# Delta-rule attention, two expert stages and a dense stage on one core: the first two chunks inverted one at a time, x reordered by on-chip transfers, four raw weight buffers at the start

## The chip, the core and the metric

The kernel runs on one core of one Trainium2 chip. The metric is the device time of one execution in microseconds (us). The core has five engines that run their own instruction lists and wait for each other by semaphores: PE (matrix products, its weight loads shown apart as PEld), DVE, ACT and POOL (elementwise work) and SP, which here only issues transfers. 16 DMA engines carry the transfers.

## The reference

Three stages follow one another. The first is a recurrence over 768 time steps for 4 x 8 heads of width 48; the second is a mixture of eight experts whose weights per token come from eight rounds of row and column scaling; the third is a dense product.

```python
for t in range(S):                     # S = 768, state is D x D per head, D = 48
    y[:, :, t] = einsum(q[:, :, t], state)
    v_old = einsum(state, kt)          # kt is k[t] over its norm plus 1e-6
    state = state + bt * outer(kt, vt - v_old)
x = y as (3072 tokens, 384)
P = exp(x @ w_gate - max); 8 rounds of row and column scaling
out = sum over 8 experts e of P[:, e] * (relu(x @ w1[e]) @ w2[e])     # 384 -> 1024 -> 384
result = ((out @ a1) * (out @ a2)) @ w3 @ w_out                      # 384 -> 1024 -> 1024 -> 384
```

## The kernel before

**Phases.** The time axis is cut into 12 chunks of 64 steps, c = 0 to 11. In phase A (about the first 405 us) the chunks are solved one after the other and expert 0 is computed for each chunk's 256 tokens as soon as its x is there. Phase B does experts 1 to 7 in three passes over the tokens, phase C the dense stage; both need nothing of a chunk's order beyond x itself.

**One chunk of phase A.** `prep_k` (L508) forms the Gram products of k on PE, squares k on ACT, and on DVE sums the squares and turns beta into beta over the squared norm (L521 to L538, tiles `nrm`, `bm`, `nv`). The recurrence inside a chunk is a unit triangular 64 x 64 system per head. `invert` (L588) inverts two chunks (a pair j) at once: DVE transposes `a` so that each partition holds one 32 x 32 block (L599), multiplies by beta, does forward substitution for the 8 x 8 blocks by 14 short instructions (L609 to L614), joins them by the pairs of a product and a sum in `prod` (L616 to L626, a 512-element product and a 512-element sum at a time, later 1024), and transposes back. For the pairs j = 1 to 5 it goes on up to 32 x 32 (L670, L672) and `tt_make` joins the halves to 64 x 64 on PE. For j = 0 it stops at 16 x 16 blocks, and `substitute` (L729) forms on PE the matrix R that is left over; in `seq` three products with R (written `rv`, PE reading `xst`) and a sum on DVE after each (`u<-b,vs`) finish the solution. Before the change, chunks 0 and 1 come out of one inversion.

**From the chunk to expert 0.** `seq` (L787) multiplies the solution into y (`pt,u` on PE), and ACT copies y to the tile `xst` in on-chip memory. Its rows are per head. Two transfers then write it to the DRAM tensor `xs_d`, which is in the order of the model's features, and `xload` (L779) reads it back as three blocks of 128 features:

```python
self.dma(lambda b=b: T["xs_d"][c].rearrange("h (j q e) t -> q e (h j) t", q=2, e=D)[b], ...)   # two of them
self.dma(raw, lambda: self.T["xs_d"][c].rearrange("h (k p) t -> p (h k) t", p=128), ...)       # and back
```

ACT copies that to `xr` as a high part, and POOL or DVE subtracts to get the low part. `e0` (L916) does expert 0 with it: 72 products of `xr` by `wA` and 72 of `hA` by `wA` for a chunk. `xr` has two buffers, so chunk c + 2 can be loaded only once the 72 `xr` products of chunk c are done.

**Expert 0's weights.** `load_w` (L984) loads eight blocks into two raw buffers in turn (`yr` and `wraw`), ACT copies each to the high part in `wA`, and POOL subtracts the low part in one instruction of 768 elements.

**The order of the work.** It is not written out by hand. `Plan.order` places every operation by its priority, a cost and latencies, and each engine then runs its list strictly in that order. While PE has nothing to do before the first chunk's expert work, the planner puts in products of a zero tile `wz` (up to 400, `setup`), which compute nothing. The fillers stop once an expert 0 product with a priority from 200 on is placed. A transfer is issued by SP in SP's order, so one that waits holds up the next.

Of the kernel before, what the change touches and what calls it, by code (L numbers as in the profile page):

```python
# [20 lines left out]
D = 48  # L21
# [27 lines left out]
SUB = 2  # L49
FLAT = "p a b c d -> p (a b c d)"  # L50
# [28 lines left out]
class Plan:  # L79
# [58 lines left out]
    WARM = 20.0  # L138
    SEED = 32
    PASS_BY = .05  # L140
# [238 lines left out]
class Kernel:  # L379
# [56 lines left out]
    def setup(self):  # L436
        nc, T, g = self.nc, self.T, self.g
        n = NCH * NG
        self.open("const", "left", ones=((128, 128), F32), masks=((128, 78), F32),
# [16 lines left out]
                  asys=((128, 1056), F32), t=((128, 1056), F32), prod=((128, NP, 1024), F32), xs=((128, 256), F32), bm2=((128, 2, 32), F32), wz=((128, 384), F16),  # L456
# [14 lines left out]
        g.op({"POOL": .2}, lambda e: nc.gpsimd.memset(T["t"].rearrange("p (i x) -> p i x", x=33)[:, :, 0:1], 1.0), w=["t"], prio=-5)  # L471
        self.dma(lambda: T["wgr"], lambda: a["moe_w_gate"].rearrange("(k p) e -> p k e", p=128), 12288, [], ["wgr"], -5)
        g.op({"POOL": .2}, lambda e: nc.gpsimd.memset(T["ones"], 1.0), w=["ones"], prio=-31)
        g.op({"ACT": 1.5}, lambda e: nc.scalar.activation(out=T["nrm"][:, 1, 0:1], in_=T["ones"][:, 0:1], func=AF.Sqrt), r=["ones"], w=["n1"], prio=-30)
# [34 lines left out]
    def prep_k(self, c):  # L509
# [13 lines left out]
        if st:  # L523
            n0 = [("n0", 0), ("n0", 1)]
            bm = lambda: T["bm"][:, 32 * j:32 * j + 32]
            nv = lambda: T["nv"][:, 32 * j:32 * j + 32]
            g.op({"DVE": .1}, lambda e: nc.vector.tensor_scalar(out=nr(0), in0=nr(0), scalar1=1e-30, scalar2=None, op0=ALU.max), w=n0, prio=pr)
            g.op({"ACT": .25}, lambda e: nc.scalar.activation(out=nr(1), in_=nr(0), func=AF.Sqrt), r=n0, w=["n1"], prio=pr)
# [15 lines left out]
        if c < SUB:  # L544
            g.op({"POOL": .4}, lambda e: nc.gpsimd.memset(self.rb(c)[:, :, :, 48:64], 0.0), w=[("gm", c)], prio=-6)
# [7 lines left out]
        for hf in range(2):  # L553
# [5 lines left out]
            if c >= SUB:  # L559
                g.op({"ACT": act(256, True)}, lambda e, s=s, gs=gs, st=st: self.copy(  # L560
                    "ACT", T["g12"][:, gi, st, gs], self.ps(s, 8, 64)[:, :, 32:64], -1.0),
                    r=[s], w=[(n, gi, st, hf) for n in ("g12", "xsb0", "xsb1")], prio=pg)
            g.op({"ACT": act(256, True)}, lambda e, s=s, ss=ss, a0=a0: self.copy(
                "ACT", T["a0"][:, a0.at, ss], self.ps(s, 8, 64)[:, :, 0:32], -1.0), r=[s], w=[ak], prio=pg)
            for r in (slice(32, 64), slice(96, 128)):
                g.op({"ACT": act(256, True)}, lambda e, s=s, ss=ss, a0=a0, r=r: self.copy(
                    "ACT", T["a0"][r, a0.at, ss], self.ps(s, 8, 64)[r, :, 32:64], -1.0), r=[s], w=[ak], prio=pg)
            for i in range(3) if c < SUB else ():
                g.op({"ACT": act(128, True)}, lambda e, s=s, hf=hf, i=i: self.copy(
# [18 lines left out]
    def invert(self, j):  # L588
# [55 lines left out]
        if j == 0:  # L644
# [6 lines left out]
            for c in range(SUB):  # L651
                self.substitute(c)
# [963 lines left out]
```

## Time and profile before

| what | us |
|---|---|
| median of 3 runs (lowest, highest) | 2077.08 (2074.74, 2077.18) |
| the profiled execution, device time | 2078.16 |
| its span in the trace | 2076.4 |
| PE busy in the span | 2044.1 |
| DVE busy in the span | 1208.9 |

The span is what the profiler saw from the first to the last instruction, 1.8 us less than the device time of the same execution. Busy time of PE counts the fillers like any other product. DVE's share of the span (58%) is a mean over phases: the page's 40 slices show it at 7 to 9 tenths in the first six, which are phase A up to 311 us, and lower after them.

### The profile page before, as it was taken

Reading aid. Unit: us, or ns where it says so; the run is one execution under the profiler, and the core shown is the slowest. Engines: PE = TensorE matmul, PEld = TensorE weight load, DVE = VectorE, ACT = ScalarE, POOL = GpSimd, SP = SyncE. Lnnn points to the kernel's source line nnn. Section 1 sums busy time; section 2 is a strip of 40 time slices with the busy share of each in tenths; the row PEclk is TensorE's granted clock in tenths of the full one; section 3 lists DMA queues with packets and bytes.
Section 4 is the critical chain, followed back from the end, with each engine's and each line's share of the span. In section 5 each row is a group of like instructions: output and inputs, shape, how many; then the busy total and the mean of one; then the engine's idle time right before and its main releaser. Section 6 shows DMA issues by size and latency. Waiting matters only on the chain.

```text
span 2076.4 us, 39969 instructions
## 1 busy us (share of the span) xinstructions
PE 2044.1 (98%) x16463; PEld 1749.8 (84%) x16463; DVE 1208.9 (58%) x1947; ACT 733.1 (35%) x1438; POOL 792.4 (38%) x849
## 2 busy tenths in 40 slices
PE   7999999999999999999999999999999999999999
PEld 6898999978888888788888888788888888988888
DVE  7898882665444445756666667766666643222222
ACT  6545433343443443323333323323323322222222
POOL 1300011067666667355454454443554534200000
PEclk9999999999999999999999999999999999999999
DMA  5444323276645546755655545656546537400000
GB/s 215 133 141 130 110 73 109 72 259 234 227 173 188 212 178 223 269 174 204 220 189 175 204 152 191 239 189 208 202 164 216 188 106 208 102 31 16 16 23 24
DMA packets 166615, 331.64 MB, mean 160 GB/s; under 512 B 13409, under 2 KB 117793, under 8 KB 154913
## 3 DMA queue, kind: packets, MB, share of 16 engines
q1 hardware_dynamic: 132544, 193.82, 27.6%
q0 software_dynamic: 33888, 135.28, 19.2%
q8 instruction: 129, 2.11, 0.4%
q14 instruction: 54, 0.43, 0.1%
HBM read 235.10 MB, written 93.95 MB: 158 GB/s over the span
## 4 chain that ended last, share of the span: by engine, by line
PE 87%; DVE 5%; DMA 5%; issue 1%; POOL 1%; ACT 1%; SPq 0%; POOLq 0%; DVEq 0%; ACTq 0%
PE b L401 87%; DMA acc<-y_d 1%; DMA wo_d<-cv 1%; DVE prod L412 1%; DMA xs_d<-xst 1%; DMA xst<-xs_d 0%; DMA rawB<-in_moe_w 0%; SPq L432 0%; DMA xT<-xs_d 0%; DVE cv L415 0%; POOL acc L412 0%; DVE xs L625 0%; POOL wA L412 0%; DVE hA L415 0%; DMA xf_d<-acc 0%
## 5 line engine op out<-in xcount | busy, mean ns | idle before, releaser
L401 PE MATMUL b<-hA,wA 128*128 128x512 f32 (+1 forms) x2367 | 508.3, 353 | 5.0 <-DVE hA L415 5.0
L401 PEld LDWEIGHTS b<-hA,wA 128*128 128x128 f32 x2367 | 392.4, 189 | 67.5 <-DVE hA L415 6.2
L412 POOL TENSOR_TENSOR acc<-acc,tmp 128x512 f32<-128x512 f32 x252 | 335.8, 1334 | 195.3 <-DVE tmp L412 190.8
L401 PE MATMUL b<-hB,wA 128*128 128x512 f32 x1521 | 388.4, 391 | 0.2 <-DVE hB L415 0.2
L401 PEld LDWEIGHTS b<-hB,wA 128*128 128x128 f32 x1521 | 287.1, 189 | 60.5 <-DVE hB L415 0.6
L401 PE MATMUL b<-xr,wA 128*128 128x256 f32 (+1 forms) x1620 | 326.4, 335 | 1.5 <-POOL xr L412 1.5
L401 PEld LDWEIGHTS b<-xr,wA 128*128 128x128 f32 x1620 | 250.1, 189 | 33.9 <-POOL xr L412 1.7
L405 ACT ACTIVATE rt<-b 128x512 f32<-128x512 f32 x300 | 178.4, 598 | 257.5 <-PE b L401 252.2
L401 PE MATMUL b<-xT,wA 128*128 128x512 f32 x1008 | 249.9, 389 | 1.8 <-POOL wA L412 1.8
L412 DVE TENSOR_TENSOR b<-b,rt 128x512 f32<-128x512 f32 x252 | 173.4, 695 | 103.2 <-ACT rt L405 73.8
L401 PEld LDWEIGHTS b<-xT,wA 128*128 128x128 f32 x1008 | 189.0, 188 | 41.8 <-POOL wA L412 2.7
L412 POOL TENSOR_TENSOR cv<-cv 128x256 f32<-128x256 f32 (+3 forms) x179 | 131.9, 737 | 209.5 <-DVE cv L1376 115.8
L401 PE MATMUL b<-xT,wS 128*128 128x512 f32 x756 | 199.3, 390 | 1.4 <-ACT rt L405 1.4
L412 DVE TENSOR_TENSOR tmp<-b,pb 128x512 f32<-128x512 f32 x150 | 103.2, 689 | 137.9 <-PE b L401 133.6
L415 DVE SCALAR_TENSOR_TENSOR hA<-b,hA 128x512 fp32r<-128x512 f32 x215 | 144.2, 688 | 62.0 <-ACT hA L941 30.3
L401 PEld LDWEIGHTS b<-xT,wS 128*128 128x128 f32 x756 | 141.7, 188 | 31.8 <-ACT rt L405 2.2
L412 DVE TENSOR_TENSOR rt<-b,rt 128x512 f32<-128x512 f32 x48 | 33.2, 692 | 186.0 <-PE b L401 186.0
L415 DVE SCALAR_TENSOR_TENSOR hB<-b,hB 128x512 fp32r<-128x512 f32 x169 | 114.8, 686 | 32.8 <-ACT hB L1181 32.4
L412 DVE TENSOR_TENSOR tmp<-b,yr 128x512 f32<-128x512 f32 x102 | 70.2, 689 | 98.0 <-PE b L401 85.3
L412 POOL TENSOR_TENSOR wA<-rawB,wA 128x768 fp32r<-128x768 f32 (+1 forms) x49 | 88.6, 1818 | 100.1 <-DMA pb<-p_d 72.4
L405 ACT ACTIVATE cv<-cv 128x256 fp32r<-128x256 f32 x72 | 29.1, 404 | 272.1 <-DVE cv L415 272.1
L1181 ACT ACTIVATE hB<-b 128x512 fp32r<-128x512 f32 x169 | 100.1, 596 | 69.6 <-DVE b L412 67.5
(189 smaller groups left out, 2421.4 us busy)
## 6 DMA issues: line engine op xcount, KB each, us to landing
wA<-wq_d POOLq DMA_DIRECT2D x56, 1536.0 KB, 8.9
wq_d<-wA SPq DMA_DIRECT2D x28, 1536.0 KB, 7.1
wS<-ws_d POOLq DMA_DIRECT2D x56, 512.0 KB, 4.8
rawB<-in_moe_w SPq DMA_DIRECT2D x108, 192.0 KB, 3.4
ws_d<-wS SPq DMA_DIRECT2D x28, 512.0 KB, 6.6
w_d<-cv SPq DMA_DIRECT2D x112, 128.0 KB, 1.7
cvr<-in_w3T SPq DMA_DIRECT2D x32, 256.0 KB, 2.9
wS<-w_d POOLq DMA_DIRECT2D x32, 256.0 KB, 3.6
```

What stands on the lines that cost most here:

```text
L401: self.nc.tensor.matmul(*args, skip_group_check=True, **kw)
L405: self.nc.scalar.activation(out=out, in_=in_, func=AF.Copy, **({} if scale is None else {"scale": scale}))
L412: self.E[eng].tensor_tensor(out=out, in0=in0, in1=in1, op=op)
L415: self.nc.vector.scalar_tensor_tensor(out=out, in0=in0, scalar=scalar, in1=in1, op0=op0, op1=op1)
L1181: g.op({"ACT": actb(512)}, lambda e: nc.scalar.activation(out=hv(0), in_=self.ps(s, 512), func=AF.Relu), r=[s], w=[(out, 0, 0)], prio=pe)
```

## The change

- **Chunks 0 and 1.** `invert(0)` now calls a new function `blocks16` once for each of the two chunks, followed by `substitute`. For one chunk it transposes 512 elements, so that all partitions work on its 16 x 16 diagonal blocks, two 8 x 8 blocks each, and joins these by two pairs of product and sum in place of four. The norms and beta of chunks 0 and 1 are computed apart, 16 columns each, and a new small product `bq` puts masks on beta. R is now masked on DVE (`xst<-b,masks`) while it is copied out; before, ACT copied it and the masks were on the twelve small copies of the Gram products, of which four whole copies are left.
- **x.** y's 48 rows per head half are put into three blocks of 128 rows within `xst`: the heads' rows stay, and six small transfers move the fourth part (16 rows each, 16 KB) into the free rows. x is thus in another order of features; the rows of the gate's and of w1's matrices are permuted to match when the inputs are laid out. Expert 0 no longer waits for DRAM; `xs_d` is still written, for phase B.
- **Weights.** Four raw buffers at first (a third slot of `kraw` and of `vs` beside `yr` and `wraw`), issued earlier (priorities `WP`), and POOL's subtraction is cut in three pieces of 256 elements, which wait for the end of chunk 0's inversion.
- **The planner's constants** WARM, SEED, PASS_BY are others (20.0, 32, .05 before), so that the whole order is drawn anew.

```diff
-    WARM = 20.0
-    SEED = 32
-    PASS_BY = .05
+    WARM = 13.0
+    SEED = 26
+    PASS_BY = 0.02
...
+    def blocks16(self, c):
...
+        pr = -131.0 if c == 0 else 1.0
...
+        raw = lambda: T["asys"][:, 0:512].rearrange("p (i r) -> p i r", i=16)
...
+        g.op({"DVE": dve(512)}, port=True, fn=lambda e: self.tt(
+            e, v4(), v4(), T["bq"][:, 4:6, 16 * c:16 * c + 16].rearrange("p a (s o) -> p s a o", o=1).to_broadcast([128, 16, 2, 16]), ALU.mult),
+            r=[("bq", c)], w=ka, prio=pr)
+        g.op({"DVE": 1.0}, lambda e: nc.vector.transpose(
+            out=raw().rearrange("p i (a s) -> p i a s", a=2), in_=v4().rearrange("p s a i -> p i a s")), r=ka, w=["asys"], prio=pr)
+        g.op({"DVE": dve(256)}, port=True, fn=lambda e: self.tt(
+            e, am().rearrange("p i q -> p q i"), raw()[:, :, 0:16], raw()[:, :, 16:32], ALU.add), r=["asys"], w=[("F", c)], prio=pr)
+        for i in range(1, 8):
...
+                "DVE", pv(), blk(t16)[:, :, 0:i, 0:i],
...
     def invert(self, j):
+        if j == 0:
+            for c in range(2):
+                self.blocks16(c)
+                self.substitute(c)
+            return
...
         for hf in range(2):
-            g.op({"ACT": act(512, True)}, lambda e, hf=hf: self.copy(e, self.rb(c)[:, hf], self.ps(sr[hf], 8, 64)),
-                 r=[sr[hf], ("gmr", c)], w=[("R", c, hf)], prio=pr)
+            g.op({"DVE": dve(512)}, lambda e, hf=hf: self.tt(
+                e, self.rb(c)[:, hf], self.ps(sr[hf], 8, 64), T["masks"][:, 84:148].rearrange("p (o t) -> p o t", o=1).to_broadcast([128, 8, 64]),
+                ALU.mult), r=[sr[hf], ("gmr", c), "masks"], w=[("R", c, hf)], prio=pr)
...
-        for b in range(2):
-            self.dma(lambda b=b: T["xs_d"][c].rearrange("h (j q e) t -> q e (h j) t", q=2, e=D)[b],
...
+        for k_ in range(3):
+            for b in range(2):
+                r0, r1 = 64 * b + 16 * k_, 64 * b + 48
+                self.dma(lambda r1=r1, k_=k_: xv()[r1:r1 + 16, :, k_], lambda r0=r0: xv()[r0:r0 + 16, :, 3], 16384,
+                         [(xb, 0), (xb, 1)], [(xb, "m", k_, b)], pr + .5, lat=.9, cost=.4)
...
+        self.xload(lambda i: T["xr"][:, i, x.at], lambda: xv()[:, :, 0:3], xk, x, pr + .5)
+        for hh in range(2):
+            self.dma(lambda hh=hh: T["xs_d"][c, hh].rearrange("(k p) t -> p k t", p=128), lambda hh=hh: xv()[:, hh, 0:3], 196608,
+                     xk, [("xs", c, hh)], pr + .5)
...
+        for i in range(3):
+            g.op({"POOL": pool2(256)}, port=True, fn=lambda e, i=i: self.tt(
...
+                r=[(raw, 0), (raw, 1), ("w", sl, 0), ("t16e", 0)], w=[("w", sl, 1)], prio=prio)
...
+                    ring, nm = {2: (self.kraw, "kraw"), 3: (self.vring, "vs")}.get(n, (self.wraw, None))
```

Three places of the changed order follow, as the two lists have them; the numbers after the names are the tiles' numbers.

**DVE, chunk 0 from the scaled beta to the end of the inversion.** Before, for both chunks at once (the 14 short instructions and four of the pairs stand between):

```order
L538 TENSOR_TENSOR bm_98<-bm_98,nrm_100 128x32
L599 STREAM_TRANSPOSE asys_114<-a0_113 128x1024
L601 STREAM_TRANSPOSE a0_113<-bm_98 128x32
L412 TENSOR_TENSOR asys_114<-asys_114,a0_113 128x1024
L412 TENSOR_TENSOR prod_116<-t_115,asys_114 128x4
...
L645 STREAM_TRANSPOSE a0_113<-t_115 128x32x32
L412 TENSOR_TENSOR tt_94<-a0_113,bm2_118 128x16x32 x2
```

and now, for chunk 0 alone:

```order
L544 TENSOR_TENSOR bm_98<-bm_98,nrm_100 128x16
L413 TENSOR_TENSOR bq_118<-bm_98,masks_59 128x6x16
L413 TENSOR_TENSOR a0_113<-a0_113,bq_118 128x512
L615 STREAM_TRANSPOSE asys_114<-a0_113 128x512
L413 TENSOR_TENSOR asys_114<-asys_114 128x16x16
L413 TENSOR_TENSOR prod_116<-t16_119,asys_114 128x2
...
L639 STREAM_TRANSPOSE a0_113<-t16_119 128x16x2x16
L413 TENSOR_TENSOR tt_94<-a0_113,bq_118 128x16x32 x2
```

The same steps with about half the elements each; chunk 1's come again later in DVE's list, between the sums `u<-b,vs` of chunk 0, and the inversion of pair 1 starts behind them.

**SP, chunk 0's x.** Before, out to DRAM and back:

```order
L432 DMA vs_95<-in_v 128x768
L432 DMA xs_d_123<-xst_104 48x8x128 x2
L432 DMA yr_85<-in_moe_w1 128x3x128
L432 DMA yr_85<-in_moe_w2 128x384
L432 DMA kraw_89<-in_k 128x768
L432 DMA xst_104<-xs_d_123 128x6x128
```

and now, six within on-chip memory, with the DRAM copy behind them:

```order
L433 DMA vs_95<-in_v 128x768
L433 DMA wraw_121<-in_moe_w1 128x3x128
L433 DMA wraw_121<-in_moe_w2 128x384
L433 DMA kraw_89<-in_k 128x768
L433 DMA xst_104<-xst_104 16x2x128 x6
L433 DMA kraw_89<-in_k 128x768
L433 DMA vs_95<-in_v 128x768
L433 DMA kt_91<-in_kT 128x1024
L433 DMA xs_d_124<-xst_104 128x3x128 x2
```

The round trip is gone from the path to expert 0, and three loads that wait for other engines stand directly ahead of the six.

**PE, the three products with R of chunk 1.** Before, expert 0 products stand between them:

```order
L401 MATMUL b3_139<-vs_95,xst_104 64x48 x16
L401 MATMUL b6_142<-vs_95,xst_104 64x48 x16
L401 MATMUL b2_138<-xr_81,wA_73 128x256 x6
...
L401 MATMUL b3_139<-u_97,xst_104 64x48 x16
L401 MATMUL b6_142<-u_97,xst_104 64x48 x16
L401 MATMUL b2_138<-xr_81,wA_73 128x256 x3
```

and now the second and the third stand together:

```order
L402 MATMUL b6_143<-masks_59,yr_85 128x8 x2
L402 MATMUL b5_142<-u_97,xst_104 64x48 x16
L402 MATMUL b6_143<-u_97,xst_104 64x48 x16
L402 MATMUL b3_140<-u_97,xst_104 64x48 x16
L402 MATMUL b5_142<-u_97,xst_104 64x48 x16
L402 MATMUL b6_143<-xr_81,wA_73 128x256 x6
```

Each of the four waits for a sum of DVE, and PE has nothing else in its list between them. In PE's list as a whole every product of before is there again in the same number; only the fillers are 161 in place of 190.

## Rows read from the trace of the kernel before

**Rows 1.** Windows, two stretches: PE, PEld, DVE, ACT, POOL busy (count), clock, DMA share, GB/s.

```profile
0.00:64.95 64.95, 50.23 (x1339) 43.07 (x1339) 50.52 (x92) 43.74 (x119) 17.14 (x21) 0.97 0.64 224
...
110.00:400.00 290.00, 284.44 (x6430) 266.88 (x6430) 215.06 (x359) 120.80 (x273) 21.05 (x24) 1.00 0.36 109
```

**Rows 2.** Windows, the fillers (tile wz) alone: PE, PEld, DVE.

```profile
0.00:64.95 64.95, 24.16 (x185) 17.94 (x185) 0.22 (x1) 0.97 0.64 224
64.95:110.00 45.05, 1.07 (x5) 0.32 (x5) 0.00 (x0) 1.00 0.31 89
```

**Rows 3.** Chain that ended last, first 70 us: start, length, what.

```profile
1.65 4.18 DMA kn<-in_kn
...
9.87 0.97 DVE nrm L521
...
13.20 1.87 DVE asys L599
...
26.12 2.07 DVE a L645
...
28.82 0.70 DVE tt L412
...
50.59 0.60 ACT xst L405
...
51.59 4.34 DMA xs_d<-xst
...
55.98 5.38 DMA xst<-xs_d
61.38 0.85 ACT xr L405
...
62.31 2.60 POOL xr L412
```

**Rows 4.** Timeline, DVE, first 90 us: start, length, line, instruction, count.

```profile
6.73 0.95 DVE L521 TENSOR_REDUCE nrm<-kn 128x16 f32<-128x768 f32 x1 [5.66 <-ACT kn L519]
...
16.66 0.17 DVE L412 TENSOR_TENSOR prod<-t,asys 128x4 f32<-128x4 f32 x1
...
20.12 0.36 DVE L613 TENSOR_REDUCE t<-prod 128x28 f32<-128x196 f32 x1
20.51 0.69 DVE L412 TENSOR_TENSOR prod<-asys,t 128x512 f32<-128x512 f32 x1
...
40.04 1.73 DVE L538 TENSOR_TENSOR bm<-bm,nrm 128x32 f32<-128x32 f32 x1
...
88.54 2.02 DVE L672 STREAM_TRANSPOSE a<-t 128x1024 f32<-128x1024 f32 x1
```

**Rows 5.** Timeline, ACT, first 25 us.

```profile
9.86 1.18 ACT L405 ACTIVATE a<-b 128x256 f32<-128x256 f32 x3
...
19.25 2.82 ACT L405 ACTIVATE vs<-vs,nv 128x48 f32<-128x48 f32 x12
```

**Rows 6.** DMA issues by line: count, KB each, median us to landing.

```profile
p_d<-tmp SPq DMA_DIRECT2D x2, 48.0 KB, 1.6
```

**Rows 7.** Windows, products with wA alone, until DVE ended x of chunks 1, 2, 4.

```profile
0.00:92.80 92.80, 14.70 (x96) 12.34 (x97) 0.00 (x0) 6.75 (x8) 15.86 (x8) 0.98 0.54 184
92.80:128.30 35.50, 20.98 (x147) 18.13 (x146) 0.00 (x0) 0.00 (x0) 0.00 (x0) 1.00 0.43 129
128.30:183.10 54.80, 33.31 (x240) 29.56 (x239) 0.00 (x0) 0.00 (x0) 0.00 (x0) 1.00 0.42 128
```

**Rows 8.** Windows, between the ends of the inversions of pairs 1 and 2.

```profile
90.56:144.90 54.34, 53.93 (x1424) 49.13 (x1418) 48.43 (x78) 27.56 (x66) 2.66 (x3) 1.00 0.41 122
```

**Rows 9.** Timeline, PE: chunk 2's y, and expert 0 undisturbed.

```profile
115.08 1.11 PE L401 MATMUL b<-pt,u 64*48 64x64 f32 x64
...
340.87 2.32 PE L401 MATMUL b<-xr,wA 128*128 128x256 f32 x18
343.03 1.24 PE L401 MATMUL b<-hA,wA 128*128 128x256 f32 x9
```

**Rows 10.** Waits of PE, whole span: who, for whom, total us, times, longest.

```profile
PE b L401 <- DVE u L412: 2.5, 1, 2.5
```

More of the change, by code (lines that the diff above doesn't have):

```diff
@@ L522, in prep_k @@
              r=[kn], w=[("n0", st)], prio=pr)
[L523 to L528, printed above, removed]
+        if st or j == 0:
+            cs = slice(16 * st, 16 * st + 16) if j == 0 else slice(0, 32)
+            n0 = [("n0", x) for x in range(2) if j or x == st]
+            n1 = [("n1", x) for x in range(2) if j or x == st]
+            bm = lambda: T["bm"][:, 32 * j:32 * j + 32][:, cs]
+            nv = lambda: T["nv"][:, 32 * j:32 * j + 32][:, cs]
+            nq = lambda i: nr(i)[:, cs]
+            g.op({"DVE": .1}, lambda e: nc.vector.tensor_scalar(out=nq(0), in0=nq(0), scalar1=1e-30, scalar2=None, op0=ALU.max), w=n0, prio=pr)
+            g.op({"ACT": .25}, lambda e: nc.scalar.activation(out=nq(1), in_=nq(0), func=AF.Sqrt), r=n0, w=n1, prio=pr)
@@ L538, in newton @@
-                v.tensor_tensor(out=bm(), in0=bm(), in1=nr(2), op=ALU.mult)
-            g.op({"DVE": 1.77}, newton, port=True, r=n0 + ["bm"], w=["n1", ("bm", j), ("nv", j)], prio=pr)
+                v.reciprocal(out=nq(2), in_=nq(1))
+                v.tensor_tensor(out=nq(2), in0=nq(2), in1=nq(0), op=ALU.mult)
+                v.tensor_tensor(out=nq(1), in0=nq(1), in1=nq(2), op=ALU.add)
+                v.tensor_scalar(out=nv(), in0=nq(1), scalar1=0.5, scalar2=1e-6, op0=ALU.mult, op1=ALU.add)
@@ L643, in invert @@
                  lambda p=p: xt(p, 8), 8, 8, 8, [("tr", p), ("x8", p)], [("t8", p)])
[L644 to L654 removed]
         rk = ["asys", "t", ("t8", 0), ("t8", 1)]
[L656 removed]
+        by_rows(0, 16, 16, ["t", ("t8", 0), ("t8", 1), ("tr", 0), ("tr", 1)])
         x16 = lambda: xt(0, 16).rearrange("p c q -> p q c")
@@ L757, in prep_q @@
         k = self.K[c]
-        sp = [self.psum.new("attn" if c else "early") for _ in range(2)]
+        sp = [self.psum.new("attn" if c > 1 else "early") for _ in range(2)]
         for hf in range(2):
@@ L828, in seq @@
                     V(hf), self.ps(sk[hf], 8, D), -1.0, V(hf), ALU.mult, ALU.add), r=[sk[hf]], w=[(v, hf)], prio=pr)
-        sy = two()
+        sy = two() if c else [self.psum.new("early") for _ in range(2)]
         if c > 0:
@@ L1586, in layouts @@
     masks[:, 64] = i >= 32
-    for b in range(3):
-        masks[:, 75 + b] = -1.0 * (i >= 16 * b + 16)
+    for b in range(4):
+        masks[:, 78 + b] = i // 16 == b
+    for b in range(2):
+        masks[:, 82 + b] = i % 32 // 16 == b
+    masks[:, 84:148] = i[:, None] // 16 < t[None, :] // 16
     masks[:, 66:74] = i[:, None] % NE == t[None, :NE]
@@ L1591, in layouts @@
                masks=masks, w3T=f(inputs["moe2_w3"].T).view(np.int64))
+    p = np.arange(128)
+    q, e = p // 64, p % 64
+    rows = np.concatenate([np.where(e < D, D * (2 * n + q) + e, D * (6 + q) + 16 * n + e - D) for n in range(3)])
     for nm in ("moe_w_gate", "moe_w1", "moe_w2", "moe2_w1", "moe2_w2", "moe2_w_out"):
         res[nm] = f(inputs[nm])
+        if nm in ("moe_w_gate", "moe_w1"):
+            res[nm] = f(np.take(inputs[nm], rows, axis=-2))
         if nm.startswith("moe2"):
```

139 lines of the change are left out of this document (82 added, 57 removed).

## The prediction

> **What bounds the kernel now.** I read the windows first. Once expert 0's products run, PE is hardly ever free: from 110 to 400 us it is busy 284.4 of 290 us, and its clock is at full speed (granted 1.00, the 2.4 GHz level) [rows 1]. From there to the end the time is PE's work and little else, so what can be won is what PE loses before. Up to 64.95 us, when expert 0 starts in earnest, PE is idle for 64.95 - 50.23 = 14.7 us [rows 1], and 24.2 us of its busy time are fillers that compute nothing, with 1.1 us more behind [rows 2]. That is **40.0 us lost**; the real work until then is 50.23 - 24.16 = 26.1 us. The order shows the same products in the same number, so the gain is 40.0 us less what PE loses after the change.
>
> What PE waits for is chunk 0's chain [rows 3]. The reader sees k arrive at 5.8 us, the second chunk's norms from 9.9, DVE's joint inversion from 13.2 to 28.2, the scaled result at 29.5, y in `xst` at 51.2, 10.2 us until it is back from DRAM at 61.4, and 0.85 and 2.6 us for the two parts of x.
>
> Behind PE stands DVE. From the end of pair 1's inversion to that of pair 2's it is busy 48.4 of 54.3 us [rows 8], so it delivers two chunks in some 54 us and not much faster. PE is therefore fed closely: when x of chunk 1 is ready (92.8 us), 96 of the 144 products that expert 0 has for chunk 0 are done; at chunk 2 (128.3 us) 243 of 288; at chunk 4 (183.1 us) 483 of 576 [rows 7]. Undisturbed, 18 products take 343.03 - 340.87 = 2.16 us, 0.12 each [rows 9]. So PE had 48, 45 and 93 products in hand, that is 5.8, 5.4 and 11.2 us, when these chunks came. A head start larger than that plus the earlier arrival of the chunk is lost again in waiting. This is the limit to watch.
>
> **The change part by part, up to chunk 0's x.**
>
> - *Norms of chunk 0 alone.* The sum that now starts the chain is at 6.73 us instead of 9.87 [rows 3, 4]: 3.1 us earlier. Square root and the eight short steps stay as long; beta is ready at 10.1 instead of 13.2 us.
> - *Inversion of one chunk.* From 13.2 to 28.2 it took 15.0 us. Now: the mask product on beta (96 elements, about 0.25), the product with it (512 elements, 0.69 as in [rows 4]), half a transposition (1.0, half of 1.87), a sum over 256 elements (0.4), 14 short steps with half the elements (3.25; with all they ran from 16.66 to 20.48 [rows 4], mostly a fixed part), two pairs at 1.4 = 2.8 instead of four, half a transposition back (1.0). That is 9.4 us. The scaled result follows 1.3 us later, at 20.8 instead of 29.5 us.
> - *From there to y.* It took 21.7 us. R's masking goes from ACT to DVE (two at 0.69) behind two `pt` products. The first product and its copies on ACT end at about 27 us. Then ACT's list sets the end: eight copies of a Gram product at 0.39 and 16 scalings of v at 0.235 [rows 5], together 6.9; three weight copies, a square and a fourth weight copy, all of 768 elements, at 0.85 [rows 3], 4.2; a small copy (0.25), and y's two copies (1.1). That ends at 39.7 us; PE's and DVE's part is done at about 37. Bounds: 37, if ACT runs early, and 43, if DVE is held up.
> - *Transfers.* Six issues on SP at 0.4 us and the landing of the last. No row shows a transfer of 16 KB; the nearest is 48 KB, 1.6 us [rows 6], and the far end is 4.34 us, the first transfer of x beside loads [rows 3]. The three loads that stand ahead on SP (`wraw`, `kraw`) wait for POOL and PE until about 38.5 and are still landing. I take 2.3 us, near the first: 2.4 + 2.3 = 4.7, between 4.0 and 6.7, against 10.2.
> - *x's two parts.* ACT 0.85 as before; the low part on DVE 0.96 instead of 2.6 on POOL. With three hand-overs PE can start at 46.6 us.
> - *POOL and DVE.* A product of 32 elements took 1.73 us while POOL subtracted weights beside it [rows 4], where the first short step takes 0.17. POOL's pieces are now a third as long, but 24 of them fall between 26 and 60 us. I add 0.4: **expert 0 starts at 47.0 us** instead of 64.95, between 44 and 52.
>
> **The sum.** Before that start PE no longer has chunk 1's `tt,xst` and `vs,tt` products and one Gram product, groups like `pt,u`, some 1.11 us each [rows 9]: 26.1 - 3.3 = 22.8 us of real work, so 24.2 us lost. Behind the start stand 18 fillers at 24.16/185 = 0.13 us [rows 2]: 2.3. The second and third product with R of chunk 1 now stand together, in four halves, each waiting for a sum that DVE does between steps of pair 1. In the old order PE waited once for such a sum, 2.5 us [rows 10]; following both lists I find two waits of 2.3 and 1.1 us, 3.4 in all (nothing at best, four times 2.5 at worst). Lost: 24.2 + 2.3 + 3.4 = 29.9. **Gain 40.0 - 29.9 = 10.1 us.** At nothing I cost the weights, whose cover is chunk 0's chain (all four buffers can land by about 24 us, while `xr` comes at 46), and the eight transfers per chunk instead of three, whose issues (about 0.4 us each) lie on SP, which waits most of the time. If the weights came late, they would be next on the path.
>
> **Does the head start survive?** DVE has more to do before pair 1: two inversions of 9.4 instead of one of 15.0 (+3.8), the second set of norms (+2), four maskings of R (+2.7), x's low parts (+1.9): some 10 to 11 us, from which the earlier start takes 3 and fewer idle stretches some more. I place the end of pair 1's inversion at 95 instead of 90.6 us [rows 4]. To keep 10.1 us, chunk 2's x has to be there at 128.3 + 5.4 - 10.1 = 123.6 us. It came 37.7 us after the inversion. Of that the transfers give back 5.5, and up to 12 go because PE's `pt,u` of this chunk, at 115.1 us [rows 9], waited in the list for products that now stand earlier. That gives 115 us. Chunk 4: inversion 54.3 us later [rows 8], 149.3; then 38.2 us as before less 5.5, 182.0, against 183.1 + 11.2 - 10.1 = 184.2. Both hold, the second by 2 us. Chunk 6 and later wait for `xr`'s buffers, that is for PE itself.
>
> The profiled execution took 2078.16 us, so the sum gives 2068.1; the median of the three runs is 1.1 us lower, and I forecast **2067.0 us**.
>
> **The rivals.**
>
> - *The whole head start* (0.20). The sums of chunk 1 come in time, and chunk 4 too: gain 13.5, 2063.6 us. For it: the sums cost PE a single wait before [rows 10]. Against: pair 1's steps lie between them.
> - *DVE eats half of it* (0.15). Pair 1's inversion ends 8 us late at 98.6 and chunk 2 keeps its old way of 37.7 - 5.5 us: 130.8, 7.2 after the need; gain 2.9, 2074.2 us. For it: DVE has only a tenth of its time free [rows 8].
> - *The six transfers pay one after the other* (0.07). If each waits for the one before, six at 1.6 us are 9.6 instead of 4.7: 4.9 us less, gain 5.2, 2071.9 us, and the on-chip way buys almost nothing over 10.2. Against: the two halves of y to DRAM, 192 KB each, were through in 4.34 us from the second's issue [rows 3], so transfers overlap. The Trainium skill, "DMA: Bandwidth & Descriptors", section "Rules for kernel authors", says to join many small transfers into one, since under 64 KB one mostly pays overhead, and its section on the anatomy of one DMA gives some 2.0 us of fixed cost (measured there for transfers that POOL issues). By that figure six in turn would be an estimated 12 us, and the gain 2.8.
> - *Slower: pair 1 is so late that PE starves* (0.08). The place is chunk 2's x. If POOL's 24 pieces and waits for PE push pair 1's inversion to 15 us late (105.6) and the old way stays, x comes at 105.6 + 32.2 = 137.8. PE would have used up all it had at 133.7 without any gain, so 4.1 us are lost: 2081.2. It decides from 11 us of lateness on. For it: one short product took 1.73 us [rows 4]. Against: only 4.5 us of lateness follow from the rows.
>
> **How the numbers follow.** Forecast 0.50, rivals 0.20, 0.15, 0.07, 0.08. A measurement tells 0.2%, 4.2 us, from no change. Faster by more: the forecast, the whole head start and most of the transfer case, 0.77; within: DVE's half and the rest, 0.16; slower: 0.07. The range goes from 2061 (start at 44 us with no waits in chunk 1) to 2077 (DVE late by 10 us), and leaves out the slower case and the far end of the best.
>
> **What would show it.** Right: expert 0's first steady products near 47 us, y in `xst` near 40, the six transfers landing within 5 us of it, `tt` scaled near 21, pair 1's inversion ending at 93 to 97, PE busy without longer gaps from 85 us on. Wrong: PE gaps before the `xr` products of chunks 2 or 4, which would mean DVE; weight copies on ACT waiting for `yr`; or a start later than 52 us.

## The result and the profile after

The changed kernel takes **2102.35 us** (median of 4 runs, 2101.03 to 2107.74) against 2077.13 for the kernel before: a ratio of 1.0130, 95% interval 1.0107 to 1.0154, 25 us slower. I had forecast 2067.0, a gain of 10 us, with slower at 0.07.

| what, us | before | after |
|---|---|---|
| span of the profiled execution | 2076.4 | 2105.9 |
| expert 0's x ready, chunk 0 | 64.9 | 49.0 |
| the same, chunks 1, 2, 3, 4 | 92.8, 128.3, 142.2, 183.1 | 88.4, 132.2, 149.7, 189.3 |
| pair 1 inverted | 90.6 | 99.1 |
| first product with `xT`, where phase A ends for PE | 414.7 | 417.1 |
| from there to the end | 1661.7 | 1688.9 |

"Ready" is the end of x's low part. Phase A lasts to 414.7 us in the kernel before by this measure, not to about 405. Expert 0 does start 16 us earlier. Yet phase A ends 2.4 us later, and 27.2 us are lost behind it, where the change does nothing. The windows of the two kernels behind phase A (PE, PEld, DVE, ACT and POOL busy with their counts, clock, DMA share, GB/s); of the kernel before:

```profile
414.68:2076.39 1661.71, 1649.91 (x7430) 1384.52 (x7428) 891.21 (x1414) 542.69 (x993) 744.02 (x799) 1.00 0.49 169
```

And of the changed kernel:

```profile
417.06:2105.95 1688.89, 1675.60 (x7430) 1387.14 (x7428) 894.48 (x1415) 543.76 (x993) 744.94 (x799) 1.00 0.49 166
```

PE is busy 25.7 us longer for the same 7430 recorded products; idle time grew by 1.5 us only. So PE waits for no one there: its products are slower. The groups by form, 500 to 1700 us (count | busy us, mean ns), show which. Before:

```profile
L401 PE MATMUL b<-hB,wA 128*128 128x512 f32 x1377 | 351.9, 391 | 0.2 <-DVE hB L415 0.2
L401 PE MATMUL b<-hA,wA 128*128 128x512 f32 x1373 | 350.3, 390 | 5.0 <-DVE hA L415 5.0
...
L401 PE MATMUL b<-xT,wS 128*128 128x512 f32 x684 | 179.9, 389 | 0.8 <-ACT rt L405 0.8
```

After:

```profile
L402 PE MATMUL b<-hB,wA 128*128 128x512 f32 x1363 | 355.7, 396 | 0.0
L402 PE MATMUL b<-hA,wA 128*128 128x512 f32 x1350 | 344.6, 390 | 0.2 <-ACT hA L1237 0.2
...
L402 PE MATMUL b<-xT,wS 128*128 128x512 f32 x666 | 179.5, 395 | 0.9 <-ACT rt L406 0.9
```

The products of `hA` keep their 390 ns, those of `hB` and `wS` take 5 to 6 ns more. (In these means `xT` and `xr` with `wA` rise as well, from 389 to 393 and 394 ns. Those are the products that ran in the changed kernel's two stretches at half clock, from 880.6 and 1334.6 us, each after PE had stood idle for some 3 us; at full clock they need 227.1 and 228.4 ns from start to start.) The timeline shows it in one row each: nine products in a row took 2.20 us in the kernel before,

```profile
600.84 2.20 PE L401 MATMUL b<-hA,wA 128*128 128x512 f32 x9
```

and in the changed kernel, with `hB`, 2.27 us:

```profile
600.90 2.27 PE L402 MATMUL b<-hB,wA 128*128 128x512 f32 x9
```

From the start of one to the start of the next (worked out from the starts in the trace, at full clock) a product takes 226.7 ns on the mean in every group before. After, it is 233.5 for `hB` with `wA` and 233.2 for `xT` with `wS`. What tells these groups apart is where their tiles lie. `hA`, `xr` and `xT` are stacked up from the left end of the on-chip memory like `wA`, `hB` and `wS` from the right. The change widens `masks`, at the left end, from 78 to 148 columns. In places that are multiples of 32 bytes this is 288 bytes more: `wA` moves from 18816 to 19104, while `hB` (170880) and `wS` (203648) stay. Before, all of them lay at the same place modulo 512.

In phase A the account of PE is this. Windows of the changed kernel:

```profile
0.00:49.00 49.00, 40.17 (x1104) 35.10 (x1104) 36.37 (x85) 35.12 (x91) 15.56 (x30) 1.00 0.72 243
49.00:100.00 51.00, 47.74 (x1032) 43.38 (x1033) 46.81 (x72) 18.61 (x44) 6.47 (x9) 1.00 0.35 111
100.00:150.00 50.00, 45.45 (x1298) 42.09 (x1297) 42.15 (x72) 24.59 (x58) 3.04 (x3) 0.90 0.32 96
126.28:136.52 10.24, 7.18 (x198) 6.76 (x199) 8.79 (x12) 6.03 (x14) 0.00 (x0) 0.50 0.64 200
```

And of its fillers alone (PE, PEld, DVE):

```profile
0.00:49.00 49.00, 18.14 (x143) 14.01 (x143) 0.22 (x1) 1.00 0.72 243
49.00:100.00 51.00, 2.48 (x18) 1.68 (x18) 0.00 (x0) 1.00 0.35 111
```

Up to 49.0 us PE loses 8.8 us of idle time and 18.1 of fillers, 27.0 where the kernel before lost 40.0 up to 64.95 [rows 1, 2]. In the next 51 us it loses 5.7. From 100 to 150 us it is idle for 4.6 us, and from 126.3 us on it runs 10.2 us at half clock (the 1.2 GHz level). It is busy for 7.2 of them, so the clock costs at most 3.6 us more; the 64 products `vs,tt` take 2.13 us there and 1.25 shortly before. Ahead of the fall PE had been idle for 1.4 of 3.3 us. The timeline of PE there:

```profile
116.33 1.25 PE L402 MATMUL b<-vs,tt 64*64 64x48 f32 x64
...
120.82 1.11 PE L402 MATMUL b<-pt,u 64*48 64x64 f32 x64
...
126.71 2.13 PE L402 MATMUL b<-vs,tt 64*64 64x48 f32 x64 [1.85 <-issue]
131.47 1.98 PE L402 MATMUL b<-kt 48*64 48x64 f32 x64 [2.63 <-DMA kt<-in_kT]
133.38 1.01 PE L402 MATMUL b<-xr,wA 128*128 128x256 f32 x3
```

It has used up expert 0's products, and until chunk 2's x comes it has only groups of the chunks left, for which it waits. In the kernel before, the `pt,u` of this chunk ran at 115.08 [rows 9]. SP in the same stretch:

```profile
123.08 4.20 SPq L433 DMA_DIRECT2D xst<-xst  x6
127.37 0.53 SPq L433 DMA_DIRECT2D kt<-in_kT  x1
```

The load of `kt` for which PE waits 2.63 us is behind the six transfers. The profiled execution's 29.5 us of span are thus 24.4 of slower products, 1.3 more of half clock and 1.5 of idle time behind phase A, and 2.4 in phase A.

### The profile page after: what moved, and what is told of

Its sections match the earlier page's. It is cut to its first block, busy times and chain, and to the rows that moved or that the text cites. A ratio compares the mean times of both kernels' runs of the same rounds, so it can differ in the third digit from the quotient of the medians.

```text
span 2105.9 us, 40056 instructions
## 1 busy us (share of the span) xinstructions
PE 2069.7 (98%) x16434; PEld 1753.0 (83%) x16434; DVE 1216.3 (58%) x1974; ACT 730.2 (35%) x1425; POOL 799.3 (38%) x870
## 4 chain that ended last, share of the span: by engine, by line
PE 87%; DMA 4%; DVE 3%; SPq 2%; POOL 1%; ACT 1%; issue 1%; POOLq 0%; ACTq 0%; DVEq 0%
PE b L402 87%; SPq L433 2%; DMA acc<-y_d 1%; DMA rawB<-in_moe_w 1%; DMA qt<-in_qT 1%; POOL wA L413 0%; DMA xst<-xst 0%; POOL acc L413 0%; DMA kt<-in_kT 0%; POOL sums L413 0%; DMA xf_d<-acc 0%; DVE xr L413 0%; DMA ws_d<-wS 0%; DVE tmp L413 0%; DVE rt L413 0%
## 5 line engine op out<-in xcount | busy, mean ns | idle before, releaser
L402 PEld LDWEIGHTS b<-hA,wA 128*128 128x128 f32 x2367 | 391.7, 189 | 66.8 <-DVE hA L416 0.8
L402 PE MATMUL b<-hB,wA 128*128 128x512 f32 x1521 | 396.8, 396 | 0.0
L402 PE MATMUL b<-xr,wA 128*128 128x256 f32 (+1 forms) x1620 | 333.5, 339 | 10.9 <-DVE b L413 6.2
L413 POOL TENSOR_TENSOR cv<-cv 128x256 f32<-128x256 f32 (+3 forms) x179 | 131.8, 736 | 213.7 <-DVE cv L1432 125.2
L402 PE MATMUL b<-xT,wS 128*128 128x512 f32 x756 | 204.0, 395 | 0.9 <-ACT rt L406 0.9
L413 DVE TENSOR_TENSOR tmp<-b,pb 128x512 f32<-128x512 f32 x150 | 103.4, 690 | 144.4 <-PE b L402 141.4
L413 DVE TENSOR_TENSOR rt<-b,rt 128x512 f32<-128x512 f32 x48 | 33.2, 692 | 189.5 <-PE b L402 189.5
```

What stands on the lines that cost most here:

```text
L402: self.nc.tensor.matmul(*args, skip_group_check=True, **kw)
L413: self.E[eng].tensor_tensor(out=out, in0=in0, in1=in1, op=op)
```

## The experiments

**Where the tiles lie.** Rival theories: the tiles' places, or the new order and traffic. Four kernels move tiles by widening the unused `padl` or `padr`; their instructions and order are those of the kernel that they come from.

```diff
-  wg=((128, 3, 2 * NE), F32R), padl=((128, 24), F32)
+  wg=((128, 3, 2 * NE), F32R), padl=((128, 32), F32)      # a_l32, and b_l32 from the kernel before
+  wg=((128, 3, 2 * NE), F32R), padl=((128, 80), F32)      # a_l512
-  self.open("edge", "right", padr=((128, 24), F32))
+  self.open("edge", "right", padr=((128, 32), F32))       # a_r32
```

> The changed kernel with 8 more unused columns (32 bytes) of padding behind the gate weights, so that wA, hA, xr and xT start at a multiple of 64 bytes again; hB and wS always did. The instructions and their order are the same. Theory (operands of a product that stand 32 bytes apart modulo 64 make each 512-column product some 7 ns longer): in the phase behind the Sinkhorn part the products of hB, wS with wA or xT go back from 231-235 ns to 227 ns from start to start; that is 18.9 us less by the sums over these classes of products, so about 2083 us. What is left over the kernel before is then phase A (+2.4 us) and the waits at the passes' ends. Rival (the planner's other order, other loads and the small transfers make the later phase slower): no difference, 2102 us.

> The same with 56 more columns (224 bytes), so that the tiles of the left side stand where they stood modulo 512 bytes in the kernel before. Theory with a period of 64 bytes: the same time as with 32 bytes, about 2083 us. With a period of 128 to 512 bytes: this one alone gives the 19 us back, and the one with 32 bytes keeps 2102 us.

> The changed kernel with 32 bytes more at the right end instead, so that hB and wS also start 32 bytes off a multiple of 64, as wA, hA, xr and xT do. Theory (what counts is how the two operands stand to each other): 227 ns everywhere again, about 2083 us. Rival (an operand 32 bytes off a multiple of 64 is slow by itself): no better than 2102 us.

> The kernel before with the 32 bytes of padding that take its left tiles off the multiple of 64 bytes, nothing else. Theory: the later phase gets the changed kernel's 231-235 ns for the same classes of products, 18.9 us more, about 2096 us. Rival (it was the change's order and traffic): 2077 us as before.

Measured: a_l32 2100.41 us, a_l512 2079.67, a_r32 2097.76, b_l32 2098.63, and the kernel before, run beside them, 2072.09. b_l32 is the clearest: 32 bytes of unused padding in the kernel before cost 1.29% (1.05 to 1.53). Moving the changed kernel's tiles back to their places modulo 512 leaves 0.34% of loss (0.18 to 0.49). So the places were shown to be the cause of the greater part, and my period of 64 bytes fell: by it a_l32 and a_r32 should have come to 2083 us. Behind phase A, a_l512 and then b_l32:

```profile
417.05:2075.30 1658.25, 1647.70 (x7430) 1383.81 (x7428) 894.17 (x1415) 542.31 (x993) 744.81 (x799) 1.00 0.49 169
```

```profile
419.28:2096.85 1677.57, 1670.33 (x7430) 1384.06 (x7428) 896.51 (x1415) 544.43 (x993) 744.99 (x799) 1.00 0.49 167
```

The same 7430 records: 1647.7 us against 1649.9 in the kernel before, and 1670.3 against 1675.6 in the changed one. A fifth kernel looks for the period: `padl` at 16 columns, and 32 unused columns above `hB`.

> The changed kernel with its tiles moved so that hB stands 128 bytes and wS 256 bytes off the left tiles (wA, hA, xr, xT) modulo 512; instructions and order the same. What is looked at is the time from start to start in the products of hB with wA and of xT or xr with wS (226.8 ns with no offset; 233.5 and 233.2 with 32; 233.3 and 229.2 with 64). Period of 128 bytes: 226.8 for both. Period of 256: more than 228 for hB with wA, 226.8 for those with wS. Period of 512 or more: more than 228 for both.

It took 2089.44 us. From start to start, `hB` with `wA` (128 bytes off) needs 231.6 ns, `xT` with `wS` (256 bytes off) 226.9. Together with the equal times at 32 (b_l32) and 288 bytes (the changed kernel) this makes the period 256.

**Parts of the change.** All from here on have the tiles at the old places. The question is why phase A gains nothing. Theory 1: DVE's additional work; theory 2: waiting for the transfers in the lists; theory 3: the order that was drawn. `b_onchip` puts the six transfers and permuted rows into the kernel before; `a_dram` puts the two writes and `xload`'s read back into the changed one; the others change constants:

```diff
-                         [(xb, 0), (xb, 1)], [(xb, "m", k_, b)], pr + .5, lat=.9, cost=.4)
+                         [(xb, 0), (xb, 1)], [(xb, "m", k_, b)], pr + .5, lat=2.6, cost=.64)   # a_lat
-    SEED = 26
-    PASS_BY = 0.02
+    SEED = 32                                                                              # a_seed
+    PASS_BY = .05
```

> The kernel before with one part of the change alone: x put in expert 0's order by the six small on-chip transfers (and the rows of the expert's and the gate's weights permuted for it), no round trip through DRAM. Its tiles stand where they stood. Theory 1 (the transfers save a little, DVE's extra work for inverting the first two chunks one by one eats the head start): x of chunk 0 comes some 3 us earlier than 64.9 us, pair 1's inversion ends by about 90 us as before, chunk 2's x stays by 128 us, and the time is within 4 us of the kernel before. Theory 2 (waiting for the transfers on ACT's and DVE's lists delays the later chunks): pair 1's inversion ends 3 us or more later than 90.6, chunk 2's x comes after 130 us, and the time is slower by 5 us or more.

> The changed kernel, tiles at the old places modulo 512 bytes, with x taken through DRAM again as before; one-by-one inversion, raw buffers and planner constants stay. Against the changed kernel at the old places (pair 1's inversion 99.1 us, chunk 2's x 131.8, phase B from 417 us, 2079.7 us): theory 1: pair 1's inversion still ends at 97 to 100 us and chunk 2's x comes at 130 to 135 us; no faster. Theory 2: pair 1's inversion back at 94 to 95 us, chunk 2's x by 126 us, and 5 us or more faster.

> The changed kernel at the old places with the planner told what the six transfers cost in the trace: 0.64 us for an issue instead of 0.4 and 2.6 us instead of 0.9 for the last landing. Theory 1: ACT's waits for the transfers (20.7 us in six) shrink, but pair 1's inversion stays at 97 us or later, and the time within 4 us of 2079.7. Theory 2: DVE's and ACT's idle time before x's parts goes into pair 1's steps, which end at 94 to 95 us, and the time drops by 5 us or more.

> The changed kernel at the old places with two constants of the planner as before (SEED 32, PASS_BY .05 instead of 26 and .02); they only draw which of PE's groups is passed over. Theories 1 and 2: pair 1's inversion within 2 us of 99, phase B from 415 to 419 us, the time within 4 us of 2079.7. Theory 3 (the order that these constants draw costs the gain): phase B from 410 us or earlier and 5 us or more faster, or as much slower, which would say that single runs of such kernels differ by their draw alone.

Later three more draws were made: `a_s19`, and `b_s12` and `b_s28` of the kernel before, which differ in SEED alone.

> The changed kernel at the old places with another draw of the planner's lists (SEED 19 instead of 26). Theory 4 (the draw decides as much as the change): phase B's start differs by more than 5 us from 417, with expert 0's start still at 47 to 52 us. Theory 1 or 2: phase B's start within 3 us of 417.

> The kernel before with another draw (SEED 12 instead of 32). Theory 4: phase B starts 5 us or more later than 414.7, as the draw of the kernel before is a good one, and the change is better than a like draw of the kernel before. If it starts within 3 us of 414.7, the draw matters little in the kernel before, and the change's own waits stay the cause.

> The kernel before with a third draw (SEED 28). As for SEED 12: theory 4 has phase B's start 5 us or more behind 414.7; without it within 3 us.

| kernel | x of chunks 0, 1, 2 | pair 1 inverted | phase A ends | median | ratio to before (95%) |
|---|---|---|---|---|---|
| before | 64.9, 92.8, 128.3 | 90.6 | 414.7 | 2077.1 | |
| b_s28 | 63.0, 95.4, 128.2 | 90.6 | 414.5 | 2076.9 | 1.0006 (0.9984 to 1.0029) |
| b_s12 | 66.8, 96.3, 126.3 | 95.5 | 426.0 | 2080.6 | 1.0017 (1.0000 to 1.0034) |
| b_onchip | 62.2, 95.9, 134.1 | 99.0 | 431.5 | 2088.1 | 1.0057 (1.0033 to 1.0081) |
| a_s19 | 49.8, 89.0, 136.6 | 99.7 | 416.0 | 2077.1 | 1.0019 (0.9998 to 1.0039) |
| a_l512 | 48.3, 88.4, 131.8 | 99.1 | 417.1 | 2079.7 | 1.0034 (1.0018 to 1.0049) |
| a_dram | 53.1, 93.4, 132.5 | 97.8 | 419.9 | 2080.8 | 1.0023 (1.0003 to 1.0043) |
| a_lat | 51.5, 91.6, 141.4 | 102.7 | 428.2 | 2086.5 | 1.0052 (1.0030 to 1.0074) |
| a_seed | 51.5, 91.0, 133.5 | 106.7 | 436.0 | 2094.9 | 1.0096 (1.0070 to 1.0121) |

Each ratio is against runs of the kernel before taken beside that kernel (medians 2072.1 to 2074.9 us), so the ratios are to be compared, not the medians. A trace is one execution, and single moments in it scatter. Five traces have the changed kernel's lists and other places of the tiles (the changed kernel, a_l512, a_l32, a_r32 and a_p): phase A ends at 417.1, 417.1, 418.0, 424.2 and 418.2 us, pair 1 at 99.1 to 104.4. The kernel before and b_l32 share theirs too, with 414.7 and 419.3. Most of the scatter is there early: chunk 0's `pt,u` begins between 37.2 and 43.3 us in the five. From chunk 0's x to pair 1's end they agree within 1 us (49.8 to 50.8). So a shift of a few us in the end of phase A shows nothing by itself.

Two things follow from the table. Two numbers of the planner move the end of phase A by 19 us (a_l512 to a_seed), so a kernel that differs in one part and in its draw cannot show the worth of the part: a_lat, a_dram and b_onchip settle nothing about theories 1 and 2. By its expectation b_onchip would speak for theory 2 and a_dram for theory 1. The three further draws are as mixed: b_s12 (426.0) is what theory 4 expected, a_s19 (416.0) and b_s28 (414.5) are not. And over all draws the pattern holds: with the change chunk 0's x comes 10 to 18 us earlier than in the kernel before and its two other draws, chunk 1's at most 8 us earlier, and chunk 2's 3 to 15 us later. The head start ends at chunk 2 in every one, and no draw with the change ends phase A earlier than 416.0.

**The same lists, with less in them.** To be free of the draw, the next kernels keep a_l512's lists, and single operations issue nothing (`c or` below skips them for chunk 1) or are moved by hand.

```diff
-                "DVE", pv(), blk(t16)...                 # 14 steps and 2 products of blocks16
+  fn=lambda e, pv=pv, i=i: c or self.tt(                 # k_less: not for chunk 1
-                self.dma(lambda r1=r1, k_=k_: xv()...    # the six transfers
+                g.op({"SP": .4}, lambda _: None, ...)    # k_notrans; k_both has both
```

> The changed kernel at the old places with every engine's list as it is, but chunk 1's inversion leaves out its 14 short steps and its two 8x8 products on DVE (the result of chunk 1 is not computed then); 7.2 us of DVE's work go by the durations from 32.47 to 41.71 us of the trace. Theory 1 (DVE's amount of work before pair 1's end sets when chunk 2 comes): pair 1's inversion ends 5 to 7 us earlier, at 92 to 94 us, chunk 2's x by 127 us, PE loses some 3 us between 100 and 150 us instead of 9.3, phase B from 407 to 411 us, time about 2072. Theory 2 (DVE and ACT wait for the transfers): the time won on DVE turns into waiting before x's low parts, pair 1's inversion stays within 2 us of 99, phase B within 2 us of 417.

> The same lists, with the six small transfers of every chunk left out (the rows that they move are not moved, so expert 0 gets other numbers). Theory 1: chunk 0's x comes some 6 us earlier, but pair 1's inversion ends no more than DVE's two waits earlier (4.6 us in all), chunk 2's x no earlier than 126 us, phase B from 412 us or later. Theory 2: phase B from 405 to 409 us and 8 us or more faster, since ACT's six waits for transfers (20.7 us) go.

> Both left out, lists otherwise the same. Theory 1 and 2 together: pair 1's inversion by 89 us, chunk 2's x by 121 us, PE loses less than 3 us between 100 and 150 us, phase B from 403 us or earlier. If it gains no more than the better of the two alone, one limit stands behind both.

k_less: expert 0's x 50.7, pair 1 101.4, chunk 2's x 134.5, phase A to 420.1, 2077.08 us, ratio 1.0011 (0.9996 to 1.0026), which overlaps a_l512's. Pair 1 is inverted 50.7 us behind chunk 0's x in both, so the 7.2 us taken off DVE moved nothing there. Yet this doesn't clear DVE. The steps left out stand ahead of x's low part, for which DVE waits in any case; behind it both traces give DVE the same work. Windows from chunk 0's x to pair 1's end, of a_l512 and then of k_less:

```profile
48.32:99.06 50.74, 46.55 (x1007) 42.45 (x1009) 45.87 (x72) 18.48 (x43) 5.69 (x7) 1.00 0.34 109
```

```profile
50.68:101.37 50.69, 46.58 (x1007) 42.46 (x1009) 45.87 (x72) 18.49 (x43) 5.69 (x7) 1.00 0.34 110
```

DVE is busy 45.87 of some 50.7 us. Theory 1 falls for the work that DVE does while it would wait; the work behind chunk 0's x no run cuts by more than 0.9 us (t_both).

k_notrans: 49.5, 98.9, 130.5, 413.5; 2069.32 us, ratio 0.9976 (0.9964 to 0.9987). Against a_l512's ratio the transfers of all chunks cost 0.6%, some 12 us, and the two intervals don't overlap. Its trace shows 3.5 us in phase A and 4 us of span. The medians differ by 10.4 us; 6.3 of these lie in which executions were profiled, 3.7 us above the median for k_notrans and 2.6 below it for a_l512. k_both: 47.5, 98.4, 130.0, 414.5; 2070.26 us, ratio 0.9981 (0.9962 to 0.9999), no more than the better of the two. That expert 0 starts no earlier without transfers is in part this scatter: chunk 0's `pt,u`, ahead of all transfers, was late in that trace. Timelines of a_l512 and of k_notrans, PE:

```profile
37.32 1.11 PE L402 MATMUL b<-pt,u 64*48 64x64 f32 x64
```

```profile
40.70 1.11 PE L402 MATMUL b<-pt,u 64*48 64x64 f32 x64
```

From there to the end of x's low part it took 11.0 us in a_l512, 8.8 in k_notrans and 7.6 in k_both. PE's list could stand in the way as well. k_less, timeline, PE:

```profile
38.55 1.81 PE L402 MATMUL b<-wz 128*128 128x256 f16 x15
40.29 1.11 PE L402 MATMUL b<-pt,u 64*48 64x64 f32 x64
...
42.05 3.01 PE L402 MATMUL b<-wz 128*128 128x256 f16 x26
44.99 1.15 PE L402 MATMUL b<-st,kt 48*64 48x48 f32 x64
```

Fillers are fixed in number, so what comes earlier may have to wait behind them. `t_both` keeps everything but moves the load of `kt` ahead of chunk 2's transfers and the low part of chunk 1's x from DVE to POOL:

```diff
+  order.insert(at, order.pop(i))          # at: the place of the first of the six transfers, i: that of kt's load
-  fn=lambda e: self.tt(e, dst(1), raw()
+  fn=lambda e: self.tt("POOL" if pr == -98.5 else e, dst(1), raw()
```

> The changed kernel at the old places, every list as it is but for two moves: on SP the load of kt that stood behind chunk 2's six transfers now stands ahead of them, and the low part of chunk 1's x goes from DVE to POOL. Theory 2 (what the change put in front of others on SP and DVE is what delays): pair 1's inversion ends 2 to 3 us earlier than 99.1, PE's wait of 2.2 us for kt at 131 us goes, phase B from 412 to 414 us, time 3 to 5 us less than 2079.7. Theory 4 (the lists as drawn put expert 0's products on PE ahead of chunk 2's groups, and no single wait decides): chunk 2's x stays at 130 us or later, phase B within 2 us of 417.

It took 2077.81 us, ratio 1.0018 (1.0003 to 1.0033); phase A ends at 419.1, pair 1 at 103.7, 52.7 us behind chunk 0's x; theory 2's gain of 3 to 5 us in phase A didn't come, and the ratio overlaps a_l512's. PE's wait for `kt` is gone, but DVE now waits for another product of chunk 1's x. Timeline of t_both, DVE:

```profile
91.28 1.21 DVE L688 TENSOR_REDUCE t<-prod 128x64 f32<-128x1024 f32 x1
97.36 0.69 DVE L416 SCALAR_TENSOR_TENSOR hA<-b,hA 128x512 fp32r<-128x512 f32 x1 [4.87 <-ACT hA L995]
97.97 1.21 DVE L688 TENSOR_REDUCE t<-prod 128x128 f32<-128x1024 f32 x1
```

The wait moved from one instruction ahead of pair 1's last steps to the next. Last, the 161 fillers were left out of a_l512 (n_a) and of k_both (n_both): `lambda e: None` in place of the product.

> The changed kernel at the old places with the same lists, but the 161 filler products left out. If the fillers only fill idle time and hold the clock: expert 0's start stays at 47 to 49 us or comes later, with more time at half clock early. If they stand in the way on PE's list: expert 0 starts up to 5 us earlier.

> The kernel with chunk 1's short steps and the six transfers left out, now without the fillers too; lists otherwise the same. In k_both the chain to expert 0's start (48.8 us) ran through fillers on PE. If the fillers ate what those two gave: expert 0 starts by 43 us, pair 1's inversion by 93, chunk 2's x by 125, and phase B by 411 us, if the clock holds. If not: expert 0 at 47 us or later and phase B within 2 us of 414.5.

n_a: expert 0's x at 50.0, more half clock (17 us of it before 58 us, where a_l512 has none), phase A to 421.9, 2085.11 us, ratio 1.0054 (1.0037 to 1.0072). The fillers are not in the way of the changed kernel; they hold the clock. What they are worth isn't shown: the interval overlaps a_l512's, and a_r32 with all its fillers ended phase A at 424.2. n_both: 48.9, 97.7, 129.3, 416.2; 2073.65 us, ratio 0.9988 (0.9969 to 1.0008). Without chunk 1's steps, transfers and fillers expert 0 starts no earlier still. Timeline of n_both, ACT:

```profile
42.16 0.88 ACT L406 ACTIVATE st<-b 128x384 f32<-128x384 f32 x2
45.71 0.84 ACT L406 ACTIVATE wA<-wraw 128x768 fp32r<-128x768 f32 x1 [2.67 <-DMA wraw<-in_moe_w]
46.46 0.82 ACT L406 ACTIVATE xr<-xst 128x768 fp32r<-128x768 f32 x1
```

y is copied by 42.3 us, and ACT then waits for a raw weight block before it may copy x. So three things end within some 4 us of each other at expert 0's start: in the changed kernel the copy of the weights at 43.8 us, the fillers on PE at 46.8, the transfers at 47.1. No version was found that does the whole work and beats the kernel before: b_s28 and a_s19 can't be told from it, and k_notrans and k_both leave out what they would need.

## Why the prediction was wrong

- *Everything behind phase A stays as it is.* Never said, but the sum rests on it: "from there to the end the time is PE's work". This is the step that failed by far the most: PE's products behind phase A took 24.4 us more. The change widens the tile `masks`, and I priced its width at nothing without a word. What the runs showed in its place: the wider tile moves the left tiles by 288 bytes against the right ones, and 32 bytes of padding alone cost the kernel before 1.29% (b_l32).
- *Chunk 0's chain.* Right in its times: beta ready 9.93 us (10.1 forecast), the scaled result 21.52 (20.8), y in `xst` 39.77 (39.7, though its terms add up to 39.5). That the last agrees so closely is luck: I had ACT's list set it, but ACT had its scalings and weight copies done at 37.23 and waited 1.12 us for a step of DVE. PE's and DVE's part, forecast for about 37, ended 1.3 us late. Timeline of the changed kernel, DVE and ACT:

```profile
9.96 0.26 DVE L413 TENSOR_TENSOR bq<-bm,masks 128x96 f32<-128x96 f32 x1
...
20.23 1.29 DVE L413 TENSOR_TENSOR tt<-a,bq 128x512 f32<-128x512 f32 x2
```

```profile
38.34 0.32 ACT L406 ACTIVATE xs<-t 128x64 f32<-128x64 f32 x1 [1.12 <-DVE t L625]
38.68 1.09 ACT L406 ACTIVATE xst<-b 128x512 f32<-128x512 f32 x2
...
47.15 0.84 ACT L406 ACTIVATE xr<-xst 128x768 fp32r<-128x768 f32 x1 [3.31 <-DMA xst<-xst]
```

- *Transfers: 4.7 us, 4.0 to 6.7.* Too low: from the first issue at 39.80 to ACT's copy at 47.15 they took 7.35 us, chunk 2's 7.3 as well. The six issues, 2.4 us in my sum, held SP for 5.98 and 4.20 us. Over all 72 the median time from issue to landing was 2.4 us:

```profile
xst<-xst SPq DMA_DIRECT2D x72, 16.0 KB, 2.4
```

(2.6 us, as given to the planner in a_lat, is the median with the 24 larger transfers to `xs_d` counted in.) The Trainium skill, "DMA: Bandwidth & Descriptors", section "Rules for kernel authors", asks to join small transfers since below 64 KB they mostly pay overhead. These runs agree: 16 KB land in a median 2.4 us, where 48 KB took 1.6 in the kernel before [rows 6]. But the six overlap; 7.35 us is not six times that, so the rival of six in turn didn't come.
- *Expert 0 from 47.0 us (44 to 52), and what PE loses before and just behind it.* 49.0 us, lost 27.0 against 24.2; behind the start 2.5 of fillers and 3.3 idle against 2.3 and 3.4. With this alone phase A would have gained some 7 us.
- *The head start survives.* It didn't. "I place the end of pair 1's inversion at 95": 99.07. DVE was idle no less than before and did 8.5 us more work by then (82.24 against 73.70 us busy). "Up to 12 go because PE's `pt,u` waited in the list": 2.7 of it came. `pt,u` of chunk 2 stood 21.8 us behind pair 1's end (24.5 before). From it to x it took 11.4 us (13.2 before), so the transfers gave back 1.8 instead of 5.5, and x came 33.2 us behind pair 1's end (20 forecast, 37.7 before). This is where the 10 us went: at chunk 2 PE starves and its clock falls, and by chunk 7 x is ready when it was (262.2 against 263.1). I had taken the best case of a place in a list for its likeliest.
- *At nothing: weights and the eight transfers on SP.* The weights weren't on the path: ACT waits 2.46 us for a raw block until 42.99, but after that 3.31 for x. Only with the transfers gone are they next, as I had said (n_both). The transfers were: the load of `kt` stood behind six of them, and without the six of every chunk the kernel is some 12 us faster (k_notrans).
- *Rivals.* "DVE eats half" named pair 1 at 98.6 and chunk 2's x at 130.8, close to the 99.1 and 132.2 that came, but 2074.2 us. The slower case was right in its place, PE starving before chunk 2's x, but pair 1 was not as late as its 105.6. With the tiles at the old places the loss is 0.34% or some 7 us (a_l512), against its 4.1; a fall of the clock was in neither price.

What stays open: what sets chunk 2's x. It was not DVE's short steps for chunk 1, which fell into a wait, nor any one wait that was taken away. The transfers are shown to cost time, but not that they alone are to blame, and the 45.9 us of DVE's work between chunk 0's x and pair 1's end were cut by no run, but for 0.9 us in t_both. A version with a list planned on the true times of all operations was not tried.

## What to carry to other kernels

Work that a diff doesn't touch can still change speed when a tile ahead of it grows: compare the time from start to start of the same products in a steady stretch first, and keep the two operands of such a product at the same place modulo 256 bytes. Where a planner draws the order, one part undone in a new draw tests the draw; keep the lists and leave single operations out, but none whose time only turns into a wait. Compare stretches between two steps of a trace rather than moments, and medians for the whole. A head start at the front of a pipeline is worth only what its later stages can follow, so look at the second and third delivery before the first.

## What was not expected of the hardware

The time of a 128x128 by 512 product from start to start depends on how far its two operands' places differ modulo 256 bytes. The first column is how many bytes more the left tile stands away from the right one's place than in the kernel before:

| left tiles further by | modulo 256 | `hB` with `wA`, ns | `xT` with `wS`, ns | kernel |
|---|---|---|---|---|
| 0 and 512 | 0 | 226.7 and 226.8 | 226.8 | before, a_l512 |
| 32 | 32 | 233.5 | 233.2 | b_l32 |
| 288 | 32 | 233.5 | 233.2 | after |
| 320 | 64 | 233.3 | 229.2 and 229.1 | a_l32, a_r32 |
| 384 | 128 | 231.6 | | a_p |
| 256 | 0 | | 226.9 | a_p |

It is the difference, not the place: a_l32 and a_r32 have the same difference at other places and agree within 0.1 ns. But a product's own two operands are not all of it. `hA` and `wA` are both left tiles, so their difference never changes, and yet these products, which stand between those of `hB`, need 226.7 ns in the kernel before, 227.6 in the changed kernel, 229.7 in a_l32 and a_r32 and 229.5 in a_p. In the changed kernel it is only the first one behind a product of `hB` that is slow, 232.5 ns against 226.7 for the rest. What in the chip makes it so isn't shown.
